# Weight conversion with a bit mask, block sums in the second pass and a plain last pair: one change to a fused attention and feed-forward kernel

## The chip, the cores and the metric

The kernel runs on one core of one Trainium2 chip. The metric is the device time of one execution in microseconds (us). The core has five engines with a queue each, and they run side by side: PE (TensorE, the matmuls; its weight loads are counted apart as PEld), DVE (VectorE), ACT (ScalarE), POOL (GpSimd) and SP (SyncE, which issues the DMAs). An instruction waits in its engine's queue until the semaphores it needs have been set.

## The reference, cut to what matters

```python
def _attn_ref(q, k, v):                      # each 4 x 12 x 448 x 64
    scores = scale * np.matmul(q, k.transpose(0, 1, 3, 2))
    scores = np.where(causal_mask, -1000000000.0, scores)
    attn = softmax(scores)                   # max taken off, sum + 1e-9
    return np.matmul(attn, v)

def _moe_ref(x, w_in, w_out):                # 1792 x 768, 768 x 2048, 2048 x 768
    h = x @ w_in
    g = h * np.cos(h)
    return g @ w_out
```

The attention's result, with heads and sequence swapped, is `x`. All tensors are drawn afresh as random numbers by the setup. The two weights come to the kernel as 64-bit words, and the kernel makes 32-bit floats of them itself.

## The kernel before, in words

**Precision.** Every operand of a feed-forward matmul is split into a high part (type fp32r) and the rest, the low part. A product is three matmuls: high by high, high by low, low by high. The high part is a cast on ACT, the low part a subtraction on POOL (`split`, L529 and L530; for weights L121 and L122).

**Attention** comes first, with an order written out by hand. It leaves `x` in SBUF: tokens 0 to 1023 in `xa`, the other 768 in `xb`. Beside it the first four weight chunks are converted and the first 512-token block of the feed-forward part is begun.

**Feed-forward part (`moe`).** The 2048 hidden columns are 16 chunks of 128, taken in 8 groups of two (`g`). For a group and a token block, `m1` makes two tiles of h (18 matmuls of 128x512 each, L513 to L515) and g = h cos h from them: ACT L518 (to an integer), DVE L519, ACT L520 and L521, DVE L522. The second layer is issued one step later (`flush` of the step before), so that the first-layer matmuls of the next block stand ahead of it. Only two h tiles and three output tiles (`o`) fit in PSUM; a tile is free when DVE or ACT has read it. From here on the tile scheduler, not the program text, sets the order of each queue.

- **Pass one** works on two token blocks of 512 (`xa`). Here `m2a` is the second layer: per 128 tokens 12 matmuls of 384 columns (L569), which DVE adds to `acc` (L555; L553 in the first group). In the same pass the other 28 weight chunks are converted, two per step (`convert_next`): load `st`, DVE L107 and L110 (exponent and sign bits moved into place), ACT L113 (a square, for the underflow test), DVE L116 (low bits) and L120 (zero if the square is too small), ACT L121 (high part), POOL L122 (low part). The parts are stored to DRAM (`w_in_d`, `w_out_d`), since pass two needs them again. For each pair of `w_out` chunks, `spill_out` also makes the four sums of blocks that pass two multiplies with: POOL L140, ACT L146, POOL L147, and eight stores.
- **Pass two** works on tokens 1024 to 1791 as blocks of 512 and 256 (`xb`). The second layer is a Strassen-Winograd product: of a 2 by 2 split in blocks, 7 products in place of 8. `factors` makes the sums of g blocks (POOL L597, splits L529 and L530), `m2b` the 7 products (L657) into `acc5` (512 tokens) or `acc2` (256). After the products of the last group, `after` combines the seven accumulators (L624 on DVE and POOL) and the results are stored.

DMAs all go through SP's queue. The weight tiles are in two sets, by the parity of the group; `wo_all` is a double buffer of the seven `w_out` blocks of a group, filled by one DMA (`reload_out`).

Of the kernel before, what the change touches and what calls it, by code (L numbers as in the profile page):

```python
# [9 lines left out]
F32 = mybir.dt.float32  # L10
# [3 lines left out]
U32 = mybir.dt.uint32  # L14
# [6 lines left out]
def kernel(  # L21
# [29 lines left out]
    W_MIN2 = 1.265625 * 2.0**-30  # L51

# [15 lines left out]
    w_out_d = spill.tile([NG, P, 7, 2, EH], F32, name="w_out_d")  # L68
# [56 lines left out]
    def spill_in(f, w):  # L125
        for u in range(2):
            nc.sync.dma_start(out=w_in_d[f, :, u, :], in_=f32(w[u][:]))

    def spill_out(g, w, raw, pool):
        b11, b12 = (raw[0][:, e * EH : (e + 1) * EH] for e in range(2))  # L130
        b21, b22 = (raw[1][:, e * EH : (e + 1) * EH] for e in range(2))
        for u in range(2):
            nc.sync.dma_start(out=w_out_d[g, :, 0, u, :], in_=f32(w[0][u][:, 0:EH]))
            nc.sync.dma_start(
                out=w_out_d[g, :, 1:3, u, :], in_=f32(w[1][u][:]).rearrange("p (e n) -> p e n", e=2)
            )

        def total(a, b):
            t = pool.tile([P, EH], F32, tag="tr", bufs=3, name="tr")
            nc.gpsimd.tensor_tensor(t, a, b, op=ALU.subtract)  # L140
            return t

        def put(n, t):
            th = pool.tile([P, EH], F32R, tag="th", bufs=2, name="th")
            tl = pool.tile([P, EH], F32R, tag="tl", bufs=2, name="tl")
            nc.scalar.copy(th, t)  # L146
            nc.gpsimd.tensor_tensor(tl, t, f32(th), op=ALU.subtract)  # L147
            nc.sync.dma_start(out=w_out_d[g, :, n, 0, :], in_=f32(th[:]))
            nc.sync.dma_start(out=w_out_d[g, :, n, 1, :], in_=f32(tl[:]))

        t3 = total(b22, b12)
        put(6, t3)
        t1 = total(b12, b11)
        put(4, t1)
        t2 = total(b22, t1)
        put(5, t2)
        put(3, total(b21, t2))
# [383 lines left out]
    def moe(ring, early):  # L541
        with (
# [14 lines left out]
            def m2a(g, t0, n, gs):  # L557
                for c in range(n // P):
# [4 lines left out]
                    for fi in range(2):  # L563
                        wh, wl = ring[1, 2 * g + fi]
                        gh, gl = gs[fi]
                        terms += [(gh, wh), (gh, wl), (gl, wh)]
                    for x, (a, w) in enumerate(terms):
                        for e in range(2):
                            nc.tensor.matmul(  # L569
                                o[:, e, 0:EH], lhsT=a[:, cs], rhs=w[:, e * EH : (e + 1) * EH],  # L570
                                start=(x == 0), stop=(x == 5),
                            )
                    add(g, acc[:, i], o[:, :, 0:EH])
                    if g == NG - 1:
                        nc.sync.dma_start(
                            out=out[i * P : (i + 1) * P, :], in_=acc[:, i].rearrange("p e n -> p (e n)")
                        )
# [37 lines left out]
            ORDER = [0, 5, 6, 4, 1, 3, 2]  # L615

            def m2b(g, t0, n, ops, wo, acc):
                h = n // 2
                nb = h // P
                last = g == NG - 1  # L620
                a = lambda k: acc[k - 1]

                def plus(d, b, eng=nc.vector):
                    eng.tensor_tensor(d, d, b, op=ALU.add)  # L624

                def store(d, r, e):
                    nc.sync.dma_start(
                        out=out[t0 + r * h : t0 + (r + 1) * h, e * EH : (e + 1) * EH].rearrange(
                            "(b p) n -> p b n", p=P
                        ),  # L630
                        in_=d,
                    )

                def after(i):
                    k = i + 1
                    if k == 1:
                        plus(a(2), a(1), nc.gpsimd)
                        plus(a(6), a(1))
                    elif k == 6:
                        plus(a(7), a(6))  # L640
                        plus(a(3), a(6), nc.gpsimd)
                    elif k == 7:
                        plus(a(4), a(7))
                    elif k == 5:
                        plus(a(3), a(5))
                        plus(a(5), a(7), nc.gpsimd)
                        store(a(5), 1, 1)
                    elif k == 2:
                        store(a(2), 0, 0)
                    elif k == 4:  # L650
                        store(a(4), 1, 0)
                    else:
                        store(a(3), 0, 1)
# [8 lines left out]
                if nb == 2:  # L662
                    for i in ORDER:
# [4 lines left out]
                        if last:  # L668
                            after(i)
# [158 lines left out]
```

## Time and profile before

| what | value |
|---|---|
| median of 3 runs | 692.94 us (691.65 to 693.1) |
| profiled execution, own time | 693.67 us |
| its span, first to last instruction | 691.9 us |
| PE busy, share of the span | 645.2 us, 93% |
| DVE busy | 503.7 us, 73% |
| POOL busy | 408.2 us, 59% |
| ACT busy | 377.8 us, 55% |
| DMA moved | 117.14 MB, 169 GB/s over the span |
| mean granted TensorE clock | 0.971 of full speed |

The shares are means over stages with different limits, so the kernel is to be read stage by stage: attention up to about 184 us, pass one to about 497 us, pass two after it. PE's share counts matmuls at half clock as busy too.

### The profile page before, as it was taken

How to read it: one execution, taken by the hardware profiler on the slowest of the kernel's cores; microseconds unless marked ns; L12 is line 12 of the kernel's file. 1: busy time of each engine (PE TensorE's matmuls, PEld its weight loads, DVE VectorE, ACT ScalarE, POOL GpSimd, SP SyncE). 2: the span in 40 equal slices, each digit the busy share in tenths (PEclk: the TensorE clock that was granted, in tenths of full speed). 3: DMA queues.
4: the chain of work that ended last, by engine and by line, in shares of the span. 5: the costliest groups of instructions: out<-in, count | busy, mean ns of one | idle time of the engine just before them, and what ended most of it. 6: DMA issues, size and time to landing. Idle time of an engine off the chain costs nothing.

```text
span 691.9 us, 11407 instructions
## 1 busy us (share of the span) xinstructions
PE 645.2 (93%) x3763; PEld 552.3 (80%) x3763; DVE 503.7 (73%) x1027; ACT 377.8 (55%) x913; POOL 408.2 (59%) x424
## 2 busy tenths in 40 slices
PE   8999999999799968899697989999999999999993
PEld 6676767676588857788596979999999999999993
DVE  5788888898386999998969786343355665565577
ACT  6898989998445445545353544322334534544450
POOL 3665666566157979788484747311436535744576
PEclk9999999999989989989998999999999999999998
DMA  5555556551366569776765652407836236524403
GB/s 132 119 122 142 141 127 166 133 139 47 105 215 216 176 228 307 230 255 196 261 210 204 202 207 91 161 1 270 312 102 249 99 154 251 203 101 200 160 1 136
DMA packets 112954, 117.14 MB, mean 169 GB/s; under 512 B 71936, under 2 KB 100096, under 8 KB 111872
## 3 DMA queue, kind: packets, MB, share of 16 engines
q1 hardware_dynamic: 111008, 115.96, 51.6%
q10 hardware_dynamic: 1888, 0.46, 0.3%
q8 instruction: 30, 0.49, 0.3%
q14 instruction: 28, 0.23, 0.1%
HBM read 76.28 MB, written 40.11 MB: 168 GB/s over the span
## 4 chain that ended last, share of the span: by engine, by line
PE 62%; DVE 18%; POOL 9%; issue 5%; DMA 4%; ACT 1%; SPq 0%; POOLq 0%; DVEq 0%
PE o L657 11%; PE h L513 7%; PE h L514 7%; PE o L569 7%; PE h L515 7%; PE bk L390 7%; PE sc L295 5%; PE sc L366 4%; DVE ct L110 4%; DVE ct L107 3%; DVE ct L116 3%; PE bk L304 3%; PE bk L268 3%; POOL tr L140 3%; DVE acc L555 2%
## 5 line engine op out<-in xcount | busy, mean ns | idle before, releaser
L555 DVE TENSOR_TENSOR acc<-acc,o 128x768 f32<-128x768 f32 (+1 forms) x136 | 122.7, 911 | 49.6 <-PE o L657 29.1
L530 POOL TENSOR_TENSOR gl<-r,gh 128x512 fp32r<-128x512 f32 (+1 forms) x56 | 64.6, 1154 | 65.5 <-ACT gh L529 59.5
L122 POOL TENSOR_TENSOR wl<-ct,wh 128x768 fp32r<-128x768 f32 (+1 forms) x40 | 68.9, 1729 | 52.3 <-ACT wh L121 52.3
L344 POOL TENSOR_TENSOR pb<-pb,stat 128x768 f32<-128x768 f32 (+2 forms) x72 | 73.9, 1040 | 41.8 <-ACT T L278 19.3
L513 PE MATMUL h<-xa,wh 128*128 128x512 f32 x192 | 77.8, 405 | 12.7 <-DVE r L522 12.7
L569 PE MATMUL o<-wh,gh 128*128 128x384 f32 x256 | 69.0, 351 | 18.1 <-DVE acc L555 17.0
L519 DVE SCALAR_TENSOR_TENSOR r<-ni,h 128x512 f32<-128x512 int32 (+1 forms) x64 | 39.6, 618 | 62.8 <-ACT ni L518 54.7
L326 ACT ACTIVATE pb<-pb,stat 128x384 f32<-128x384 f32 (+1 forms) x144 | 72.5, 512 | 15.0 <-DVE stat L312 15.0
L514 PE MATMUL h<-xa,wh 128*128 128x512 f32 x192 | 77.8, 405 | 0.0
L515 PE MATMUL h<-xa,wl 128*128 128x512 f32 x192 | 77.2, 402 | 0.0
L597 POOL TENSOR_TENSOR sm<-r 128x256 f32<-128x256 f32 (+1 forms) x32 | 19.3, 603 | 94.0 <-DVE r L522 94.0
L518 ACT ACTIVATE ni<-h 128x512 int32<-128x512 f32 (+1 forms) x64 | 34.6, 541 | 68.6 <-PE h L515 68.6
L569 PE MATMUL o<-wl,gh 128*128 128x384 f32 x256 | 68.3, 349 | 0.0
L569 PE MATMUL o<-wh,gl 128*128 128x384 f32 x256 | 67.8, 347 | 0.0
L569 PEld LDWEIGHTS o<-wh,gh 128*128 128x128 f32 x256 | 48.1, 196 | 23.3 <-DVE acc L555 20.0
L514 PE MATMUL h<-xb,wh 128*128 128x512 f32 (+1 forms) x192 | 64.7, 337 | 0.0
L515 PE MATMUL h<-xb,wl 128*128 128x512 f32 (+1 forms) x192 | 64.7, 337 | 0.0
L513 PE MATMUL h<-xb,wh 128*128 128x512 f32 (+1 forms) x192 | 64.6, 337 | 0.0
L312 DVE CUSTOM_DVE_ANT_0 pb<-sc,mask 128x384 f32<-128x384 f32 (+1 forms) x144 | 52.9, 418 | 14.8 <-PE sc L295 14.8
L657 PE MATMUL o<-wo_all,gh 128*128 128x384 f32 x224 | 56.4, 337 | 0.9 <-DVE acc L555 0.9
L520 ACT ACTIVATE r<-r 128x512 f32<-128x512 f32 (+1 forms) x64 | 37.0, 578 | 36.1 <-DVE r L519 36.1
L513 PEld LDWEIGHTS h<-xa,wh 128*128 128x128 f32 x192 | 37.7, 196 | 21.7 <-DVE r L522 10.0
(98 smaller groups left out, 1595.1 us busy)
## 6 DMA issues: line engine op xcount, KB each, us to landing
wo_all<-w_out_d SPq DMA_DIRECT2D x8, 2688.0 KB, 10.0
st<-in_moe_w_in_dram SPq DMA_DIRECT2D x14, 768.0 KB, 4.9
st<-in_moe_w_out_dram SPq DMA_DIRECT2D x14, 768.0 KB, 5.3
w_in_d<-wh SPq DMA_DIRECT2D x16, 384.0 KB, 5.2
w_in_d<-wl SPq DMA_DIRECT2D x16, 384.0 KB, 3.3
w_out_d<-th SPq DMA_DIRECT2D x32, 192.0 KB, 3.3
w_out_d<-tl SPq DMA_DIRECT2D x32, 192.0 KB, 2.8
wh<-w_in_d SPq DMA_DIRECT2D x16, 384.0 KB, 8.9
```

What stands on the lines that cost most here:

```text
L122: nc.gpsimd.tensor_tensor(wl, tf, f32(wh), op=ALU.subtract)
L312: nc.vector.tensor_tensor_reduce(out=dst, in0=src, in1=m, scale=-1.0, scalar=3.0e38, op0=ALU.add, op1=ALU.min, accum_out=st[:, 0, n : n + 1],)
L326: nc.scalar.activation(dst, dst, AF.Exp, scale=-1.0, bias=st[:, 0, n : n + 1], accum_out=st[:, 1, n : n + 1],)
L344: nc.gpsimd.tensor_tensor(dst, dst, r.to_broadcast(list(dst.shape)), op=ALU.mult)
L390: nc.tensor.matmul(o[heads(j), kc * P : S], lhsT=vn[:, kc, heads(j)], rhs=pm[:, kc, j, kc * P : S], start=(kc == 0), stop=(kc == NB),)
L513: yield nc.tensor.matmul(hv, lhsT=wh[:, f], rhs=x[:, 0, cc, t], start=(cc == 0), stop=False)
L514: yield nc.tensor.matmul(hv, lhsT=wh[:, f], rhs=x[:, 1, cc, t], start=False, stop=False)
L515: yield nc.tensor.matmul(hv, lhsT=wl[:, f], rhs=x[:, 0, cc, t], start=False, stop=(cc == NCC - 1))
L530: nc.gpsimd.tensor_tensor(lo, r, f32(hi), op=ALU.subtract)
L555: nc.vector.tensor_tensor(d, d, o, op=ALU.subtract)
L569: nc.tensor.matmul(o[:, e, 0:EH], lhsT=a[:, cs], rhs=w[:, e * EH : (e + 1) * EH], start=(x == 0), stop=(x == 5),)
L657: nc.tensor.matmul(o, lhsT=ops[i][u][:, b * P : (b + 1) * P], rhs=wo[:, i, v, :], start=(x == 0), stop=(x == 2),)
```

## The change

It has four parts.

- **Conversion (28 weights of pass one).** `convert_whole` takes the place of `convert_weight`. ACT makes a mask tile `mk` from the high word by three activations (L138, L139, L140): its 32 bits are those of a number just under 2, 0x3FFFFFFF, or zero where the weight is too small. DVE then needs three instructions: shift and mask (L142), low bits (L145), sign and top bits (L148). L107, L113 and L120 go for these weights. The high and low parts stay a cast on ACT (L152) and a subtraction on POOL (L153). `mk` has one buffer.
- **Block sums.** `spill_out` is gone from pass one. The converted chunk itself is stored (`raw_d`), reloaded in pass two (`reload_raw`), and `block_sums` makes the four sums of groups 0 to 6 there: POOL L707, ACT L708, DVE L709. A `reload_out` is three DMAs.
- **First `add` of an accumulator**: on ACT (L557) where it was on DVE (L553).
- **Last group of pass two**: eight plain products with the `m2a` of pass one, 72 matmuls of 384 columns where there were 63. `combine` (L651, all on POOL) brings the seven accumulators together before the last products are added, so that only an add and a store follow a chunk. The last chunk of the output is done and stored in two halves.

Lines move: L519, L522, L529, L530, L555, L569, L597 and L657 of before are L523, L526, L533, L534, L559, L575, L606 and L630 after.

```diff
-    def spill_out(g, w, raw, pool):
...
+    def convert_whole(st, w, pool):
+        wh, wl = w
+        lo32, hi32 = st[:, :, 0], st[:, :, 1]
+        hif = f32(hi32)
+        m = pool.tile([P, DM], F32, tag="mk", bufs=1, name="mk")
+        nc.scalar.activation(m, hif, AF.Identity, scale=SMALL, bias=edge[:, 0:1])
+        nc.scalar.activation(m, m, AF.Sign, bias=edge[:, 1:2])
+        nc.scalar.activation(m, m, AF.Copy, scale=ONES)
+        t = pool.tile([P, DM], U32, tag="ct1", bufs=3, name="ct")
+        nc.vector.scalar_tensor_tensor(
+            t, hi32, 3, m.bitcast(U32), op0=ALU.logical_shift_left, op1=ALU.bitwise_and
+        )
+        nc.vector.scalar_tensor_tensor(
+            t, lo32, 29, t, op0=ALU.logical_shift_right, op1=ALU.bitwise_or
+        )
+        nc.vector.scalar_tensor_tensor(
+            t, hi32, 0xC0000000, t, op0=ALU.bitwise_and, op1=ALU.bitwise_or
+        )
+        tf = f32(t[:])
+        nc.scalar.copy(wh, tf)
+        nc.gpsimd.tensor_tensor(wl, tf, f32(wh), op=ALU.subtract)
+        return tf
...
             def add(g, d, o):
                 if g == 0:
-                    nc.vector.tensor_scalar(d, o, -1.0, None, op0=ALU.mult)
+                    nc.scalar.activation(d, o, AF.Copy, scale=-1.0)
...
-            ORDER = [0, 5, 6, 4, 1, 3, 2]
...
+            def combine(a):
+                def plus(d, b):
+                    nc.gpsimd.tensor_tensor(a[d - 1], a[d - 1], a[b - 1], op=ALU.add)
+
+                plus(2, 1)
+                plus(6, 1)
+                plus(7, 6)
+                plus(3, 6)
+                plus(3, 5)
+                plus(5, 7)
+                plus(4, 7)
...
-                raw[key] = convert_weight([staged.pop(key)], ring[key], mo, bufs=3)
-                kind, f = key
-                if kind == 0:
-                    spill_in(f, ring[key])
-                elif f % 2:
-                    spill_out(f // 2, [ring[1, f - 1], ring[key]], [raw[1, f - 1], raw[key]], mo)
+                t = convert_whole(staged.pop(key), ring[key], mo)
+                spill_halves((w_in_d, w_out_d)[key[0]], key[1], ring[key])
+                if key[0]:
+                    spill_raw(key[1], t)
...
+            def reload_raw(g):
+                t = raws[g] = mo.tile([P, 2, DM], F32, tag="st1", bufs=2, name="wr")
+                nc.sync.dma_start(out=t, in_=raw_d[g])
+
+            def block_sums(g):
+                wo = wo_all[:, g % 2]
+                t = raws.pop(g)
+                b11, b12 = (t[:, 0, e * EH : (e + 1) * EH] for e in range(2))
+                b21, b22 = (t[:, 1, e * EH : (e + 1) * EH] for e in range(2))
+
+                def put(i, a, b):
+                    t = mo.tile([P, EH], F32, tag="tr", bufs=3, name="tr")
+                    nc.gpsimd.tensor_tensor(t, a, b, op=ALU.subtract)
+                    nc.scalar.copy(wo[:, i, 0, :], t)
+                    nc.vector.tensor_tensor(wo[:, i, 1, :], t, f32(wo[:, i, 0, :]), op=ALU.subtract)
+                    return t
+
+                put(6, b22, b12)
+                t2 = put(5, b22, put(4, b12, b11))
+                put(3, b21, t2)
...
-                    if u == 0 and g + 1 < NG:
+                    if u == 0 and not last:
                         reload_out(g + 1)
+                        if g + 1 < NG - 1:
+                            block_sums(g + 1)
+                        if g + 2 < NG - 1:
+                            reload_raw(g + 2)
...
+                    if last:
+                        if n == 512:
+                            combine([acc5[:, i] for i in range(7)])
+                            rows = [acc5[:, a : a + 2, b] for a in (1, 3) for b in range(2)]
...
+                        pend = (m2a, g, t0, n, gs, ws, rows)
```

What the scheduler makes of it is seen in the order of the instructions on an engine. A row is the line, the operation, output and inputs by their names in the program, and the shape.

The first place is DVE's queue in pass one around the last adds of `m2a` for group 1 and the first token block (`ct` is a weight under conversion, `st` its loaded words, `mk` the mask, `acc` the accumulator, `o` a PSUM output, `r` the cosine's tile). Before:

```order
L107 TENSOR_SCALAR ct<-st 128x768
L110 SCALAR_TENSOR_TENSOR ct<-st,ct 128x768
L555 TENSOR_TENSOR acc<-acc,o 128x768
L116 SCALAR_TENSOR_TENSOR ct<-st,ct 128x768
L120 SCALAR_TENSOR_TENSOR ct<-st,ct 128x768
L107 TENSOR_SCALAR ct<-st 128x768
L519 SCALAR_TENSOR_TENSOR r<-ni,h 128x512
L110 SCALAR_TENSOR_TENSOR ct<-st,ct 128x768
L116 SCALAR_TENSOR_TENSOR ct<-st,ct 128x768
L522 SCALAR_TENSOR_TENSOR r<-r,h 128x512
```

After:

```order
L142 SCALAR_TENSOR_TENSOR ct<-st,mk 128x768
L526 SCALAR_TENSOR_TENSOR r<-r,h 128x512
L145 SCALAR_TENSOR_TENSOR ct<-st,ct 128x768
L559 TENSOR_TENSOR acc<-acc,o 128x768
L148 SCALAR_TENSOR_TENSOR ct<-st,ct 128x768
L559 TENSOR_TENSOR acc<-acc,o 128x768
L142 SCALAR_TENSOR_TENSOR ct<-st,mk 128x768
L145 SCALAR_TENSOR_TENSOR ct<-st,ct 128x768
L148 SCALAR_TENSOR_TENSOR ct<-st,ct 128x768
L523 SCALAR_TENSOR_TENSOR r<-ni,h 128x512
```

A weight takes three rows of DVE where it took four, and all three read two tiles in SBUF. In the whole queue, 43 adds of `m2a` (L553, L555) stand ahead of the last conversion before; after, 36 on DVE and 8 on ACT do.

The second place is ACT's queue at the same point of pass one (`wh` with a number is the high part of one weight, `th` that of a block sum, `gh` that of g, `edge` two constants). Before:

```order
L121 CAST wh_3189<-ct 128x768
L520 ACTIVATE r<-r 128x512
L521 ACTIVATE r<-r 128x512
L113 ACTIVATE st<-st 128x768
L529 CAST gh<-r 128x512
L121 CAST wh_3201<-ct 128x768
L146 CAST th<-tr 128x384
L113 ACTIVATE st<-st 128x768
L146 CAST th<-tr 128x384
```

After:

```order
L152 CAST wh_3295<-ct 128x768
L524 ACTIVATE r<-r 128x512
L138 ACTIVATE mk<-st,edge 128x768
L525 ACTIVATE r<-r 128x512
L139 ACTIVATE mk<-mk,edge 128x768
L522 ACTIVATE ni<-h 128x512
L533 CAST gh<-r 128x512
L140 ACTIVATE mk<-mk 128x768
L524 ACTIVATE r<-r 128x512
L525 ACTIVATE r<-r 128x512
L138 ACTIVATE mk<-st,edge 128x768
L533 CAST gh<-r 128x512
```

The casts of block sums are gone and three mask activations stand where one square stood; the mask of the next weight is begun before the high part of the one before (the cast `wh_3311` comes three rows further on). The whole queue of ACT holds two ACT_TABLE_LOAD rows before, and the same two after.

The third place is POOL's queue at the end of the program (`fl` and `gl` are low parts of g factors, `sm` sums of g blocks). Before:

```order
L597 TENSOR_TENSOR sm<-r 128x128
L530 TENSOR_TENSOR fl<-r,fh 128x128 x2
L530 TENSOR_TENSOR fl<-sm,fh 128x128
L597 TENSOR_TENSOR sm<-sm,r 128x128
L624 TENSOR_TENSOR acc_5298<-acc_5298 128x768
L530 TENSOR_TENSOR fl<-sm,fh 128x128
L597 TENSOR_TENSOR sm<-r,sm 128x128
L530 TENSOR_TENSOR fl<-sm,fh 128x128 x2
L624 TENSOR_TENSOR acc_5298<-acc_5298 128x768
L624 TENSOR_TENSOR acc_5301<-acc_5301,acc_5299 128x384
L624 TENSOR_TENSOR acc_5302<-acc_5302,acc_5299 128x384
L624 TENSOR_TENSOR acc_5300<-acc_5300 128x384
```

After:

```order
L651 TENSOR_TENSOR acc_5160<-acc_5160 128x768 x3
L651 TENSOR_TENSOR acc_5161<-acc_5161 128x384
L651 TENSOR_TENSOR acc_5160<-acc_5160 128x768
L534 TENSOR_TENSOR gl<-r,gh 128x512
L651 TENSOR_TENSOR acc_5162<-acc_5162,acc_5161 128x384
L651 TENSOR_TENSOR acc_5160<-acc_5160 128x768
L651 TENSOR_TENSOR acc_5162<-acc_5162,acc_5161 128x384
L651 TENSOR_TENSOR acc_5164<-acc_5164,acc_5161 128x384
L534 TENSOR_TENSOR gl<-r,gh 128x256 x2
L651 TENSOR_TENSOR acc_5160<-acc_5160 128x768
L651 TENSOR_TENSOR acc_5162<-acc_5162,acc_5163 128x384
```

The sums and splits of the last factors are gone from the end of the queue; the combining adds (`acc_5160` is `acc5`, the others are `acc2`) stand among the splits of the last plain g tiles. Behind the rows shown come two more adds of 128x384.

## Rows read from the trace of the kernel before

**Rows 1.** Windows: us, busy us of PE, PEld, DVE, ACT, POOL; PEclk, DMA share, GB/s
```profile
200.50:410.00 209.50, 184.86 (x869) 165.46 (x868) 186.32 (x181) 100.94 (x159) 159.99 (x103) 0.93 0.68 227
410.00:496.90 86.90, 84.77 (x432) 77.18 (x431) 39.08 (x50) 32.02 (x54) 30.72 (x28) 1.00 0.47 172
496.90:660.50 163.60, 163.60 (x937) 152.85 (x936) 94.96 (x129) 71.90 (x178) 84.14 (x151) 1.00 0.43 167
660.50:691.90 31.40, 20.16 (x121) 18.61 (x119) 24.27 (x32) 7.93 (x21) 22.39 (x26) 0.91 0.21 76
```

**Rows 2.** Waits of PE, 200 to 410 us: total us, times, longest
```profile
PE o L569 <- DVE acc L555: 14.9, 6, 4.1
```

**Rows 3.** Chain of waits, 420 to 500 us: start, us, what (of five such periods)
```profile
424.36 6.26 PE o L569 x36
...
431.09 2.09 PE o L569 x12
...
490.65 6.26 PE o L569 x36
```

**Rows 4.** Timeline of PE at the first second-layer matmul of pass one
```profile
200.47 0.51 PE L569 MATMUL o<-wh,gh 128*128 128x384 f32 x2
```

**Rows 5.** Windows of 10 us in pass one, columns as in rows 1
```profile
250.00:260.00 10.00, 9.67 (x33) 8.64 (x34) 9.97 (x11) 4.53 (x7) 6.10 (x5) 0.69 0.60 194
```

**Rows 6.** DVE by line, 205 to 410 us: count, busy us, mean ns, idle before
```profile
L116 DVE SCALAR_TENSOR_TENSOR ct<-st,ct 128x768 uint32<-128x768 uint32 x25 | 34.4, 1378 | 0.2
L110 DVE SCALAR_TENSOR_TENSOR ct<-st,ct 128x768 uint32<-128x768 uint32 x24 | 33.8, 1409 | 0.3
L120 DVE SCALAR_TENSOR_TENSOR ct<-st,ct 128x768 f32<-128x768 f32 x25 | 33.5, 1342 | 0.7
L555 DVE TENSOR_TENSOR acc<-acc,o 128x768 f32<-128x768 f32 x32 | 29.9, 943 | 0.8 <-PE o L569 0.8
L107 DVE TENSOR_SCALAR ct<-st 128x768 uint32<-128x768 uint32 x24 | 27.0, 1125 | 7.6 <-POOL wl L122 7.2 <-POOL gl L530 0.3
L519 DVE SCALAR_TENSOR_TENSOR r<-ni,h 128x512 f32<-128x512 int32 x21 | 14.3, 679 | 8.8 <-ACT ni L518 8.8
```

**Rows 7.** Timeline of DVE and POOL: start, us, engine, line, operation
```profile
192.13 0.96 DVE L110 SCALAR_TENSOR_TENSOR ct<-st,ct 128x768 uint32<-128x768 uint32 x1
...
202.07 2.48 DVE L110 SCALAR_TENSOR_TENSOR ct<-st,ct 128x768 uint32<-128x768 uint32 x1
...
201.69 2.04 POOL L710 TENSOR_TENSOR wf<-wh,wl 128x768 f32<-128x768 f32 x1
```

**Rows 8.** POOL by line, 420 to 500 us, columns as in rows 6
```profile
L530 POOL TENSOR_TENSOR gl<-r,gh 128x512 fp32r<-128x512 f32 x8 | 10.3, 1292 | 36.7 <-ACT gh L529 30.7 <-issue 6.0
L147 POOL TENSOR_TENSOR tl<-tr,th 128x384 fp32r<-128x384 f32 x4 | 4.1, 1024 | 0.1
L122 POOL TENSOR_TENSOR wl<-ct,wh 128x768 fp32r<-128x768 f32 x2 | 3.6, 1842 | 1.7 <-ACT wh L121 1.7
```

**Rows 9.** ACT by line, 205 to 410 us, columns as in rows 6
```profile
L113 ACT ACTIVATE st<-st 128x768 f32<-128x768 f32 x25 | 23.0, 919 | 38.1 <-DVE ct L110 38.1
L121 ACT CAST wh<-ct 128x768 fp32r<-128x768 f32 x24 | 19.8, 832 | 26.7 <-DVE ct L120 22.4 <-PE h L514 3.3 <-PE o L569 1.0
...
L520 ACT ACTIVATE r<-r 128x512 f32<-128x512 f32 x20 | 12.6, 629 | 10.8 <-DVE r L519 10.8
```

**Rows 10.** Chain of waits, after 655 us, columns as in rows 3
```profile
663.81 0.12 PE h L513
```

**Rows 11.** POOL by line, 660 to 692 us, columns as in rows 6
```profile
L624 POOL TENSOR_TENSOR acc<-acc 128x768 f32<-128x768 f32 x3 | 6.3, 2088 | 0.0
```

**Rows 12.** Timeline around 660.5 us (PE) and the last computation (POOL)
```profile
660.50 0.51 PE L657 MATMUL o<-wo_all,fh 128*128 128x384 f32 x2
...
687.70 1.00 POOL L624 TENSOR_TENSOR acc<-acc 128x384 f32<-128x384 f32 x1 [2.48 <-DVE acc L624]
```

More of the change, by code (lines that the diff above doesn't have):

```diff
@@ L51 @@
     W_MIN2 = 1.265625 * 2.0**-30
+    SMALL = 0.47 * 2.0**15
+    MAGIC = 1.5 * 2.0**23
+    ONES = 2.0 - 2.0**-23
     wu_in = w_in.bitcast(U32)
@@ L67 @@
     w_in_d = spill.tile([NFC, P, 2, DM], F32, name="w_in_d")
-    w_out_d = spill.tile([NG, P, 7, 2, EH], F32, name="w_out_d")
+    w_out_d = spill.tile([NFC, P, 2, DM], F32, name="w_out_d")
+    raw_d = spill.tile([NG, P, 2, DM], F32, name="raw_d")
+    edge = keep.tile([P, 2], F32, name="edge")
+    nc.vector.memset(edge[:, 0:1], MAGIC)
+    nc.vector.memset(edge[:, 1:2], -MAGIC)
     def x_part(t0, n):
@@ L123, in convert_weight @@
             return tf
-    def spill_in(f, w):
-        for u in range(2):
-            nc.sync.dma_start(out=w_in_d[f, :, u, :], in_=f32(w[u][:]))
-    def spill_out(g, w, raw, pool):
[L130 to L157, printed above, removed]
@@ L562, in m2a @@
                     terms = []
-                    for fi in range(2):
-                        wh, wl = ring[1, 2 * g + fi]
-                        gh, gl = gs[fi]
+                    for (wh, wl), (gh, gl) in zip(ws, gs):
                         terms += [(gh, wh), (gh, wl), (gl, wh)]
[L567 to L571, printed above, removed]
-                            )
[L573 to L577, printed above, removed]
+                    steps = [(x, e) for x in range(6) for e in range(2)]
+                    end = (i + 1) * P == NT
+                    if end:
+                        steps = [(x, e) for e in range(2) for x in range(6)]
+                    for x, e in steps:
+                        a, w = terms[x]
+                        nc.tensor.matmul(
+                            o[:, e, 0:EH], lhsT=a[:, cs], rhs=w[:, e * EH : (e + 1) * EH],
+                            start=(x == 0), stop=(x == 5),
+                        )
+                    d = accs[c]
+                    for es in (slice(0, 1), slice(1, 2)) if end else (slice(0, 2),):
+                        add(g, d[:, es], o[:, es, 0:EH])
+                        if g == NG - 1:
+                            nc.sync.dma_start(
+                                out=out[i * P : (i + 1) * P, :].rearrange("p (e n) -> p e n", e=2)[:, es],
+                                in_=d[:, es],
+                            )
             def factors(n, gs):
@@ L613, in factors, with m2b @@
                 return ops
-            ORDER = [0, 5, 6, 4, 1, 3, 2]
[L617 to L653, printed above, removed]
+            PAIRS = [(0, 5), (1, 2), (3, 4), (6,)]
+            def m2b(g, t0, n, ops, wo, accs):
                 def product(o, i, b):
@@ L660, in product @@
                         )
-                if nb == 2:
-                    for i in ORDER:
+                if n == 512:
+                    for i in range(7):
                         o = out_pair()
@@ L666, in m2b @@
                             product(o[:, b, 0:EH], i, b)
-                        add(g, acc[i], o[:, :, 0:EH])
-                        if last:
-                            after(i)
-                else:
-                    for p in range(0, 7, 2):
-                        two = ORDER[p : p + 2]
+                        add(g, accs[:, i], o[:, :, 0:EH])
+                else:
+                    for two, d in zip(PAIRS, accs):
                         o = out_pair()
@@ L675, in m2b @@
                             product(o[:, j, 0:EH], i, 0)
-                        if last or len(two) == 1:
-                            for j, i in enumerate(two):
-                                add(g, acc[i], o[:, j : j + 1, 0:EH])
-                                if last:
-                                    after(i)
-                        else:
-                            add(g, acc_pair[p // 2], o[:, :, 0:EH])
+                        k = len(two)
+                        add(g, d[:, 0:k], o[:, 0:k, 0:EH])
+            def combine(a):
[8 more added lines that the diff above has]
+                plus(4, 7)
             staged = {}
@@ L686, in moe @@
             staged[todo[0]] = load_weight(*todo[0], mo)
-            raw = {}
             conv = list(todo)
```

64 lines of the change are left out of this document (47 added, 17 removed).

## The prediction

> **What bounds the kernel now.** I read the windows first, cut where the work changes [rows 1]. From 496.9 to 660.5 us PE is busy for 163.60 of 163.60 us at full clock: pass two is bound by PE. From 200.5 to 410 us it is busy for only 184.86 of 209.5 us at a granted clock of 0.93, while DVE stands at 186.32 and POOL at 159.99. From 410 to 496.9 PE is at 84.77 of 86.9. After 660.5 come 31.4 us in which PE works for 20.16.
>
> The waits say who holds PE in pass one: output banks that DVE has not yet added, 14.9 us in six waits [rows 2]. DVE in turn is full of conversions there: three kinds of SCALAR_TENSOR_TENSOR of 1.34 to 1.41 us, a TENSOR_SCALAR of 1.125, and adds of 0.943 [rows 6].
>
> What pass one would take at PE's pace is read where nothing waits. Four periods lie between the blocks at 424.36 and 490.65 us [rows 3], so one is 16.57 us. Its second layer is 48 matmuls of 384 columns in 6.26 + 2.09 = 8.35 us, 0.174 us each; the first layer of 512 tokens has the other 8.22 us. From the first second-layer matmul at 200.47 us [rows 4] to 490.65 + 6.26 = 496.91 PE does 16 second-layer steps but for the last quarter of one, and 15 first-layer steps (14 of pass one, one of pass two): 15.75 x 8.35 + 15 x 8.22 = 254.8 us. It took 296.4. So **41.6 us are lost to waits** in pass one. PE's idle time in the two windows is 24.6 + 2.1 = 26.7 us of them; the other 14.9 are matmuls at a lower clock after such gaps, as from 250 to 260 us, where the clock is 0.69 (a mix of 1.2 and 2.4 GHz) right after PE had waited [rows 5]. A wait that goes gives back more than its length.
>
> **Conversion and block sums: what DVE and POOL have left in pass one.** In the order, 44 adds stand ahead of the last conversion, that is 11 second-layer steps, so at PE's pace the 28 weights must fit in 11 x 16.57 = 182 us, 6.51 us each. Some are begun before 200 us, so this counts high.
>
> POOL first, since DVE's times hang on it. Gone are the sums: 28 low parts alone took 37.9 us (28 x 1.35, or 1.02 where POOL worked beside a lighter DVE [rows 8]), and the totals about as much again. Left are 28 x 1.842 + 22 x 1.292 [rows 8], and two 128x768 adds for the first spill of about 1.85: 84 us of 182, 46%, where it was 159.99 of 209.5, 76% [rows 1].
>
> The same DVE instruction took 0.96 us at 192.13 us, away from POOL's work, and 2.48 us beside a POOL addition of 128x768 [rows 7]; the three forms mean 1.376 us [rows 6]. If the excess over 0.95 follows POOL's share, it falls to 0.426 x 46 / 76 = 0.26, so 1.21 us an instruction and 3.6 us a weight. The rest of DVE is 36 adds of 0.943 (the eight first ones are ACT's now) and 44 steps of the cosine of 0.68: 64 us, 2.3 a weight. Sum 5.9 us. Before, DVE was busy for 0.89 of the window while it was the bound [rows 1]; at that share a weight takes 6.6 us against 6.51, that is 3 us over 28 weights.
>
> ACT takes on work: three activations of 0.919 (as L113) and a cast of 0.832 [rows 9] are 3.6 us a weight; 88 activations of the cosine and splits of about 0.63, and 8 first adds of about 0.83 (by the cast of that size) are 62 us, 2.2 a weight. Sum 5.8 of 6.51 us, 89%. That is covered, but ACT and DVE now hand each weight to and fro, both near nine tenths.
>
> Bounds for what is still lost in pass one: 0, if PE sets the pace throughout; and, if the new instructions keep the 1.376 us, (4.13 + 2.3) / 0.89 = 7.2 us a weight, 28 x 0.7 = 20 us. I take 6, near the low end since 28 weights in 182 us count high, but not 0 because of the two engines that wait for each other. Pass one gains 41.6 - 6 = 35.6 us.
>
> Here a rule speaks against the change. The Trainium skill, page "SBUF — State Buffer", section "Who interferes with whom", says that a DVE instruction with two SBUF inputs and a GpSimd instruction that reads SBUF exclude each other, the loser being held altogether. The 2.48 us of [rows 7] agree. By it all three new instructions are exposed, the first one more than the TENSOR_SCALAR it replaces; if the exposure, not POOL's load, decided, the loss would be the 20 us above.
>
> The mask activations take their constants from a tile. The Trainium skill, page "ScalarE: Activation LUTs", section "What ACT_TABLE_LOAD costs", gives about 93 ns for each such operand; that would be 28 x 2 x 0.093 = 5.2 us of ACT over pass one, as an estimate from the page, and no row here shows it.
>
> Memory traffic does not decide it: per group 2,688 KB of blocks become 1,536 KB of halves and 768 KB of raw words, and the DMA share is 0.68 [rows 1]; in 46 us less it would be at most 0.68 x 209.5 / 182 = 0.78.
>
> **Block sums in pass two.** Per group of 23.6 us (163.6 us hold about seven) POOL gets four instructions of 1.02 us, ACT four casts and DVE four subtractions of the same size. POOL is busy for 84.14 of 163.6 us there, DVE for 94.96, ACT for 71.9 [rows 1], so on average there is room: the cover is POOL's idle half. The reload of the raw words is issued a group ahead. What could be late is the last split of a block's factors, when the scheduler places sums ahead of it: three of them would be 3 us a group, six groups. I take 0 and keep 18 us for the range. The first adds on ACT are 7 + 4 instructions in this pass, with ACT less than half busy: 0.
>
> **The tail.** The first layer of the last 512 tokens ends at 660.50 us; 31.4 us follow [rows 12, 1]. After it the changed kernel has 36 matmuls of 0.12 us [rows 10], 21 of the products before (0.174 each), and 72 plain ones: 4.3 + 3.7 + 12.5 = 20.5 us. Then one half add, under the 0.943 us of a whole one [rows 6] (0.8 taken), and a store: from the end of the last computation (687.70 + 1.00) to the end of the span were 3.2 us. Sum 24.5, so 6.9 us less than 31.4, though nine matmuls more (1.6 us) are done. What went is the time in which the last factors, products and combining adds waited for each other. POOL's combining adds come on the path if late: six of 1.84 (2.09 by [rows 11]), seven of 128x384 at 1.02, and the splits of g are some 22 us from 660.5 on, about PE's own 20.5. I take 6, with 5 to 7.
>
> **Sum.** Against the profiled run's own time: 693.67 - 35.6 - 6 = 652.1 us. (That run is 0.7 us above the median of 692.94, which I leave inside the range.)
>
> **Rivals.**
> - *DVE stays the bound of pass one.* For it: three instructions with two SBUF inputs each, POOL still 46% busy, and masks that come late add waits to DVE's queue, where the adds that free PSUM stand behind L142 (the second place of the order shows how ACT's chain is cut by the cosine). Against: DVE's work per weight falls by over a quarter. The loss is 20 us in place of 6: 666 us, and more if the clock drops again in the gaps: 660 to 670.
> - *The moved sums hold PE in pass two.* For it: POOL's queue is in order, and every sum ahead of a split delays it by 1.02 us. Against: PE waits nowhere in pass two now and POOL is idle for 79.5 of 163.6 us, 11 us a group, against 4.1 us of new work. Price 18 us: 670.
> - *The mask chain runs one weight at a time* (the other side). `mk` has one buffer; if ACT cannot begin a mask before the weight before it is through, a weight is 3 x 0.92 + 3 x 1.38 + 0.83 = 7.7 us in series, with 2.2 us of cosine between: 9.9 us. Before, the 28 weights took 182 + 41.6 = 224 us, 8.0 each. 28 x 1.9 = 53 us more in pass one, less the 6 of the tail: about 740. It is slower from 8.2 us a weight on. Against: the order begins masks ahead of the previous cast.
> - *Nothing is gained*: the same chain at just 8 us a weight and the tail held up by POOL: 690 to 695.
>
> **Chances.** PE's pace in pass one (645 to 660): 0.66. DVE still the bound (660 to 670): 0.18. Sums in the way (660 to 675): 0.08. Serial masks: 0.05, of which 0.04 slower. Nothing: 0.03. Forecast 652 us; the likeliest case has 645 to 660 by itself, and for 8 in 10 the range is 645 to 668. A difference under 0.2% can't be told from none here; faster 0.93, same 0.03, slower 0.04.
>
> **What the changed profile would show.** Right: from 200 us on PE busy in nearly all of every 10 us at a clock of 1.0; waits for L559 (the add) under 6 us in pass one; L142, L145 and L148 near 1.2 us; POOL below half in pass one; the third quarter of the last second-layer step of pass one ended at about 461 us; pass two unchanged at 163 to 164 us; about 25 us from the last 512-token first layer to the end. Wrong: DVE above 0.9 with instructions of 1.4 us (the first rival), PE waiting for a split or a block sum in pass two (the second), or DVE idle before L142 with ACT as releaser (the third). A tail that ends with POOL rows L651 would make it a little longer.

## The result and the profile after

The changed kernel took 670.74 us (median of 4 runs, 668.8 to 672.53) against 692.3 us before (4 runs). The ratio is 0.9689, with a 95% interval of 0.9658 to 0.9721: 21.6 us or 3.1% faster. The direction was right, but 652 us were forecast with a range that ended at 668, so the gain came out at about half of the 40 us promised. The profiled execution took 672.53 us by its own time, with a span of 670.7.

The windows of the changed kernel, cut at the points that answer to [rows 1]: the first second-layer matmul, the end of the third chunk of the last second-layer step of pass one (where the first 256-column matmul starts), the end of the last 512-token first layer, the end. The columns are as there.

```profile
200.30:400.00 199.70, 183.79 (x898) 162.05 (x897) 154.89 (x155) 137.57 (x197) 88.54 (x49) 0.98 0.69 231
400.00:479.70 79.70, 79.70 (x401) 71.96 (x400) 40.76 (x52) 31.19 (x53) 31.87 (x27) 1.00 0.46 162
479.70:645.20 165.50, 164.09 (x938) 152.43 (x937) 97.47 (x138) 85.62 (x208) 109.40 (x170) 1.00 0.38 125
645.20:670.70 25.50, 20.88 (x130) 20.22 (x128) 11.96 (x18) 5.71 (x12) 19.73 (x16) 0.97 0.26 93
```

The cut points come from these lines of PE's timeline, the two below from the changed kernel:

```profile
200.31 0.51 PE L575 MATMUL o<-wh,gh 128*128 128x384 f32 x2
479.74 0.28 PE L517 MATMUL h<-xb,wh 128*128 128x256 f32 x1
...
645.21 0.51 PE L630 MATMUL o<-wo_all,fh 128*128 128x384 f32 x2
```

and this one from the kernel before:

```profile
496.76 0.28 PE L513 MATMUL h<-xb,wh 128*128 128x256 f32 x1
```

Stage by stage, for one work content of 254.8 us in pass one:

| stage | before | after | forecast for after |
|---|---|---|---|
| pass one, first to last cut | 296.3 us | 279.4 us | 260.8 us |
| of it lost to waits | 41.5 us | 24.6 us | 6 us |
| pass two | 163.7 us | 165.5 us | 163.7 us |
| tail | 31.4 us | 25.5 us | 25.4 us |

So the tail came out as forecast, pass two is 1.8 us longer, and almost the whole miss, 18.6 us, lies in pass one. DVE is no longer the bound there: 154.89 of 199.7 us, 0.78, where it was 0.89 [rows 1]. POOL has 0.44. PE nevertheless stands still for 15.9 us of the first window. What PE waited for in the changed kernel from 180 to 500 us, and then ACT, DVE and SP's queue from 190 to 400 us, each in a fence of its own (total us, times, longest):

```profile
PE h L517 <- DVE r L526: 11.5, 7, 4.0
PE o L575 <- DVE acc L559: 7.6, 6, 1.6
```

```profile
ACT mk L138 <- DMA st<-in_moe_w_out_dram: 26.9, 11, 5.5
ACT mk L138 <- DMA st<-in_moe_w_in_dram: 15.3, 9, 3.2
```

```profile
DVE ct L142 <- ACT mk L140: 14.5, 7, 4.4
DVE r L526 <- ACT r L525: 13.1, 7, 3.0
```

```profile
SPq L96 <- DVE ct L148: 57.7, 13, 10.8
```

Read from the bottom: SP's queue waits for the third DVE instruction of a weight before it issues a load; ACT's first mask activation waits 42.2 us in 20 waits for such loads; DVE waits for ACT's masks and cosines; PE waits for the cosine (L526), which has not yet freed an h tile. One turn of this loop, from the chain of waits (start, us, what):

```profile
380.88 1.65 DVE ct L148
...
382.59 5.34 DMA st<-in_moe_w_out_dram
...
388.01 1.01 ACT mk L138
...
389.74 0.50 ACT ni L522
390.24 0.77 ACT mk L139
...
391.05 0.63 ACT r L524
391.68 0.74 ACT mk L140
...
392.51 0.96 DVE ct L142
```

The load is issued within 0.1 us of L148's end and takes 5.34 us. ACT, in whose queue L138 comes next, does nothing for 5.53 us, and the cosine activation L522, whose h tile PE finished at 382.6 us, stands behind it until 389.6. DVE's timeline shows when this weight is through:

```profile
397.77 0.94 DVE L148 SCALAR_TENSOR_TENSOR ct<-st,ct 128x768 uint32<-128x768 uint32 x1
```

The buffer was held from 388.01 to 398.71, 10.7 us, after a load of 5.4. With two buffers two weights pass per turn: (10.7 + 5.4) / 2 = 8.0 us a weight in this turn. Over all 28 weights a buffer is held for 9.2 us on the mean from L138's start to L148's end (6.2 to 11.7), and from there to the first activation of the weight that takes the buffer next it is 6.1 us: (9.2 + 6.1) / 2 = 7.7. The order of SP's queue is not what delays the loads: of the 26 that had to wait for a buffer, 25 were issued within 0.5 us of the L148 that gave it back, the last after 1.4 us. Over pass one the first and the last L138 stand at 191.3 and 396.9 us, 27 weights apart: 7.6 us each, where PE's pace asked for 6.51.

### The profile page after: what moved, and what is told of

Same layout as the page of the kernel before. It is cut to its first block, busy times and chain, and to the rows that moved or that the text cites. A ratio compares the mean times of both kernels' runs of the same rounds, so it can differ in the third digit from the quotient of the medians.

```text
span 670.7 us, 11327 instructions
## 1 busy us (share of the span) xinstructions
PE 641.3 (96%) x3772; PEld 545.4 (81%) x3772; DVE 461.5 (69%) x995; ACT 427.6 (64%) x974; POOL 358.3 (53%) x378
## 4 chain that ended last, share of the span: by engine, by line
PE 64%; DVE 11%; ACT 11%; DMA 11%; issue 2%; POOL 1%; SPq 0%; DVEq 0%; ACTq 0%; POOLq 0%
PE o L630 11%; PE o L575 8%; PE h L517 7%; PE h L518 7%; PE h L519 7%; PE bk L394 7%; DMA st<-in_moe_w_in_dram 6%; PE sc L299 5%; PE sc L370 4%; DVE ct L145 3%; DMA st<-in_moe_w_out_dram 3%; PE bk L308 3%; PE bk L272 3%; ACT mk L138 2%; DVE ct L142 2%; DVE ct L148 2%
## 5 line engine op out<-in xcount | busy, mean ns | idle before, releaser
L559 DVE TENSOR_TENSOR acc<-acc,o 128x768 f32<-128x768 f32 (+1 forms) x129 | 117.8, 924 | 54.8 <-PE o L630 35.7
L534 POOL TENSOR_TENSOR gl<-r,gh 128x512 fp32r<-128x512 f32 (+1 forms) x57 | 67.1, 1179 | 122.9 <-ACT gh L533 71.0
L153 POOL TENSOR_TENSOR wl<-ct,wh 128x768 fp32r<-128x768 f32 x28 | 55.6, 1992 | 50.7 <-ACT wh L152 47.4
L519 PE MATMUL h<-xa,wl 128*128 128x512 f32 x192 | 77.5, 404 | 0.0
L575 PE MATMUL o<-wh,gh 128*128 128x384 f32 x256 | 66.0, 338 | 8.4 <-DVE acc L559 7.6
L523 DVE SCALAR_TENSOR_TENSOR r<-ni,h 128x512 f32<-128x512 int32 (+1 forms) x64 | 39.5, 617 | 48.7 <-ACT ni L522 47.3
L522 ACT ACTIVATE ni<-h 128x512 int32<-128x512 f32 (+1 forms) x64 | 34.6, 540 | 48.3 <-PE h L519 47.4
L575 PE MATMUL o<-wl,gh 128*128 128x384 f32 x256 | 65.2, 335 | 0.0
L575 PE MATMUL o<-wh,gl 128*128 128x384 f32 x256 | 65.1, 335 | 0.0
L519 PE MATMUL h<-xb,wl 128*128 128x512 f32 (+1 forms) x192 | 64.9, 338 | 0.0
L526 DVE SCALAR_TENSOR_TENSOR r<-r,h 128x512 f32<-128x512 f32 (+1 forms) x64 | 39.4, 618 | 36.7 <-ACT r L525 35.9
L138 ACT ACTIVATE mk<-st,edge 128x768 f32<-128x768 f32 x28 | 28.0, 1000 | 46.9 <-DMA st<-in_moe_w_out_dram 26.9
L575 PEld LDWEIGHTS o<-wh,gh 128*128 128x128 f32 x256 | 46.3, 188 | 13.8 <-DVE acc L559 10.5
```

Source lines behind the costliest of these rows:

```text
L153: nc.gpsimd.tensor_tensor(wl, tf, f32(wh), op=ALU.subtract)
L519: yield nc.tensor.matmul(hv, lhsT=wl[:, f], rhs=x[:, 0, cc, t], start=False, stop=(cc == NCC - 1))
L534: nc.gpsimd.tensor_tensor(lo, r, f32(hi), op=ALU.subtract)
L575: nc.tensor.matmul(o[:, e, 0:EH], lhsT=a[:, cs], rhs=w[:, e * EH : (e + 1) * EH], start=(x == 0), stop=(x == 5),)
```

## The experiments

Theory A is this loop: two buffers for the loaded words, each held through three mask activations and three DVE instructions, then a load. Theory B: DVE's instructions are still lengthened by POOL working beside them. Theory C: ACT and DVE wait for each other through the one mask tile and their in-order queues. The loss in pass one is worked out as in the table above; all times are medians, and the kernel before stood at 693.5 to 694.3 us beside them, so that ratios compare.

**e1, a third buffer for the loaded words.**

```diff
-        st = pool.tile([P, n, 2], U32, tag=f"st{parts}", bufs=2, name="st")
+        st = pool.tile([P, n, 2], U32, tag=f"st{parts}", bufs=3 if parts == 1 else 2, name="st")
...
-                t = raws[g] = mo.tile([P, 2, DM], F32, tag="st1", bufs=2, name="wr")
+                t = raws[g] = mo.tile([P, 2, DM], F32, tag="st1", bufs=3, name="wr")
```

> The changed kernel with three buffers in place of two for the loaded words (st). Theory A, the load loop: in the changed kernel a weight took 7.6 us because a load of 5.3 us is issued only when the third DVE instruction of the weight two places earlier has given its buffer back; the first mask activation waited 42 us for loads. Then these waits go (under 8 us in all), the loss to waits in pass one falls from 24.6 us to 5 to 10, and the median is 652 to 658 us. Theory B, DVE held by POOL: the third buffer changes little, 668 to 672 us, and the DVE instructions stay at 1.1 to 1.45 us. Theory C, ACT and DVE wait for each other through one mask buffer and in-order queues: L138 then waits for DVE in place of the load, and the time is 663 to 670.

657.69 us, ratio 0.9477 (0.9454 to 0.95), at the upper end of A's range. ACT's waits for loads are gone:

```profile
ACT mk L138 <- DVE ct L142: 31.1, 16, 4.4
...
ACT mk L138 <- DMA st<-in_moe_w_in_dram: 1.7, 1, 1.7
```

The loss in pass one is 465.41 - 200.32 - 254.8 = 10.3 us (A had 5 to 10), the weights take (378.2 - 191.3) / 27 = 6.9 us each, and pass two and the tail keep their 165.5 and 25.4 us. What the loads had held up is seen in the chain of waits. Its shares by line between 200 and 400 us, in the changed kernel and then in e1 (the view cuts its lines off there):

```profile
by line: DMA st<-in_moe_w_in_dram 17.0%; DVE ct L145 11.5%; DMA st<-in_moe_w_out_dram 11.3%; DVE ct L148 7.8%; ACT mk L138 7.1%; DVE ct L142 6.9%; ACT mk L139 6.2%; issue 5.2%; ACT mk L140 4.2%; DMA w_in_d<-wh 3.3%; DVE acc L559 3.2%; ACT r
```

```profile
by line: PE o L575 29.8%; PE h L518 9.8%; PE h L517 9.8%; PE h L519 9.7%; DVE ct L142 7.3%; DVE ct L145 5.4%; ACT mk L139 3.5%; ACT mk L138 3.3%; ACT mk L140 3.1%; issue 2.3%; DVE ct L148 2.1%; POOL wf L684 2.0%; DVE r L523 1.5%; DVE acc L5
```

In the changed kernel ten loads make 28% of the chain, 56.6 us, and the conversion's own instructions most of the rest; in e1 no load stands in it, and PE's matmuls make 59%. The DVE instructions did not become shorter; L142 and L145 became longer (1.13 and 1.44 us in the changed kernel, see e2):

```profile
L145 DVE SCALAR_TENSOR_TENSOR ct<-st,ct 128x768 uint32<-128x768 uint32 x25 | 40.3, 1613 | 0.4
L142 DVE SCALAR_TENSOR_TENSOR ct<-st,mk 128x768 uint32<-128x768 uint32 x25 | 35.8, 1432 | 12.4 <-ACT mk L140 5.5 <-POOL wl L153 3.4 <-issue 1.8
...
L148 DVE SCALAR_TENSOR_TENSOR ct<-st,ct 128x768 uint32<-128x768 uint32 x24 | 27.2, 1132 | 0.5
```

So theory B falls as the main cause: 13 us came back with the same contention. Of theory C the wait appeared that it named (31.1 us for L142, which still reads the one mask), but not the time.

**e2, the low parts by a memset on POOL.** This leaves the low part of the 28 weights out of the result.

```diff
-        nc.gpsimd.tensor_tensor(wl, tf, f32(wh), op=ALU.subtract)
+        nc.gpsimd.memset(f32(wl), 0.0)
```

> The changed kernel with the low part of the 28 weights set to zero by a memset on POOL in place of the subtraction (this leaves the low part out of the result). POOL then reads no weight tile beside DVE. Theory A: the three DVE instructions come near 0.95 us, the loop of a weight gets about 1 us shorter of some 15 for two weights, and L138 still waits over 25 us for loads: 655 to 664 us. Theory B: the waits of PE in pass one are gone, 648 to 655 us, and L138 waits for loads under 10 us. Theory C: 660 to 670.

667.76 us, ratio 0.9615 (0.9586 to 0.9644): 5 us less than the changed kernel by the ratios, less than A had expected and far from B; it lies in the range that C had. L138 still waited 23.1 + 16.0 us for loads, and the weights took (399.5 - 190.6) / 27 = 7.7 us each, no less than in the changed kernel. L142, L145 and L148 came to 1.06, 1.17 and 1.18 us in place of these of the changed kernel (205 to 380 us):

```profile
L145 DVE SCALAR_TENSOR_TENSOR ct<-st,ct 128x768 uint32<-128x768 uint32 x23 | 33.2, 1441 | 0.4
L148 DVE SCALAR_TENSOR_TENSOR ct<-st,ct 128x768 uint32<-128x768 uint32 x22 | 29.0, 1316 | 0.4
...
L142 DVE SCALAR_TENSOR_TENSOR ct<-st,mk 128x768 uint32<-128x768 uint32 x23 | 25.9, 1126 | 18.8 <-ACT mk L140 7.6 <-issue 5.3 <-POOL wl L153 3.0
```

Contention is there, and shortening it helps a little; it is not what sets the pace.

**e3, the new conversion alone** in the kernel before (sums in pass one, first adds on DVE, old last group); the definition of `convert_whole` and its constants come with it.

```diff
-                raw[key] = convert_weight([staged.pop(key)], ring[key], mo, bufs=3)
+                raw[key] = convert_whole(staged.pop(key), ring[key], mo)
```

> The kernel before with the new conversion alone (sums still in pass one, first adds on DVE, old last group). Theory A: the load loop paces it as in the changed kernel, but with POOL's sums beside it the DVE instructions stay near 1.4 us, so a weight takes 7.8 to 8.2 us: 685 to 695 us, nothing gained. Theory B: one DVE instruction less a weight, 28 x 1.125 = 31 us less of DVE: 670 to 680.

691.05 us, ratio 0.996 (0.9943 to 0.9977): 0.4%, as A had it, with 8.2 us a weight. L137, its first mask activation, waited 30.0 + 9.8 us for loads.

**e4, the changed kernel with the old conversion.**

```diff
-                t = convert_whole(staged.pop(key), ring[key], mo)
+                t = convert_weight([staged.pop(key)], ring[key], mo, bufs=3)
```

> The changed kernel with the old conversion (four DVE instructions, one square on ACT), all else as changed. Theory A: the buffer of the loaded words is held only for DVE's four instructions and not for three mask activations before them, so most of the gain is still there: 664 to 672 us, with waits of DVE for loads under 15 us. Theory B: DVE has 28 instructions more, 28 x 0.75 = 21 us: 680 to 690.

669.9 us, ratio 0.9654 (0.9627 to 0.9681), as fast as the changed kernel, as the intervals overlap; DVE waited 6.9 us for loads. The loss in pass one is 22.4 us. So the gain of pass one came from the parts that e4 keeps, the sums taken out of it and the first adds on ACT, and none from the mask.

**e5, the old last group.** `combine` and the plain pair go, the products and `after` of before take their place (`m2b_last`), and the sums are made for group 7 as well.

```diff
-                    if last:
-                        gs = [split(r, *g_tiles(n)) for r in gs]
-                    else:
-                        ops = factors(n, gs)
+                    ops = factors(n, gs)
...
-                        if g + 1 < NG - 1:
+                        if g + 1 < NG:
                             block_sums(g + 1)
...
-                        pend = (m2a, g, t0, n, gs, ws, rows)
+                        pend = (m2b_last, g, t0, n, ops, wo_all[:, g % 2], accs)
```

> The changed kernel with the old last group (seven products, combining adds behind them, sums of blocks for group 7 too). From the end of the last 512-token first layer to the end were 31.4 us before and 25.5 in the changed kernel. If the plain pair is worth that: 674 to 679 us. Rival: the first layer and the splits of the last group were only moved to another place, and the tail's gain is given back ahead of it: 669 to 673.

678.42 us, ratio 0.9772 (0.9752 to 0.9792). Against the changed kernel's 0.9689 that is 0.0083 x 693 = 5.8 us. The stretch from the last 512-token first layer to the end, in the windows of this kernel:

```profile
644.90:676.90 32.00, 20.04 (x121) 18.50 (x119) 25.17 (x33) 7.91 (x21) 20.51 (x25) 0.96 0.21 74
```

32.0 us where the changed kernel has 25.5, with pass two at 165.5 us in both. The tail's gain stands by itself.

**e6** is the kernel of e4 once more; the name under which it ran speaks of three buffers, but it has two, as its expectation says.

> The changed kernel with the old conversion, once more beside the others on the same chip: 668 to 672 us, as e4.

671.62 us in its one run.

**e7, two mask tiles** on top of e1.

```diff
-        m = pool.tile([P, DM], F32, tag="mk", bufs=1, name="mk")
+        m = pool.tile([P, DM], F32, tag="mk", bufs=2, name="mk")
...
-                    t = mo.tile([P, EH], F32, tag="tr", bufs=3, name="tr")
+                    t = mo.tile([P, DM], F32, tag="mk", bufs=2, name="tr")[:, 0:EH]
```

> Three load buffers and two mask buffers (the block sums' tiles share the mask's buffers in pass two, to make room). With three load buffers alone the first mask activation waited 31 us for L142, which still reads the one mask. Theory C in its small form, that this wait is on the path: 651 to 655 us. Rival, that PE's pace covers it: 656 to 659, with L138's wait for L142 under 8 us all the same.

670.59 us, ratio 0.9664 (0.9639 to 0.9688): both expected times missed, 13 us slower than e1. L138's wait for L142 did fall to 5.3 us, but the loss in pass one rose to 480.41 - 200.01 - 254.8 = 25.6 us. PE waited 12.6 us for adds, 6.07 us at once. DVE's timeline at that place:

```profile
281.97 0.94 DVE L142 SCALAR_TENSOR_TENSOR ct<-st,mk 128x768 uint32<-128x768 uint32 x1
282.95 0.96 DVE L145 SCALAR_TENSOR_TENSOR ct<-st,ct 128x768 uint32<-128x768 uint32 x1
283.83 0.95 DVE L142 SCALAR_TENSOR_TENSOR ct<-st,mk 128x768 uint32<-128x768 uint32 x1
284.69 2.56 DVE L148 SCALAR_TENSOR_TENSOR ct<-st,ct 128x768 uint32<-128x768 uint32 x1
287.18 0.94 DVE L559 TENSOR_TENSOR acc<-acc,o 128x768 f32<-128x768 f32 x1
```

and what PE was waiting for (the bracket: idle time before, and its releaser):

```profile
288.17 1.01 PE L575 MATMUL o<-wh,gh 128*128 128x384 f32 x2 [6.07 <-DVE acc L559]
```

With two masks the scheduler puts four instructions of two weights in a row ahead of the add that frees PE's bank. The add stands behind them, though PE waits for it from 282.1 us on. In e1 the one mask tile keeps the instructions of two weights apart. That the order costs this wait is seen here; that it accounts for the whole 15 us is not shown.

**e8, as e7 with the first add on DVE again.**

```diff
-                    nc.scalar.activation(d, o, AF.Copy, scale=-1.0)
+                    nc.vector.tensor_scalar(d, o, -1.0, None, op0=ALU.mult)
```

> As e7, with the first add of an accumulator on DVE again. In pass two of the changed kernel PE waited 1.4 us once, for a cosine behind block sums and first adds on ACT. If the first adds caused it: pass two 1 to 2 us shorter, 1 to 2 us less than e7. Rival: DVE's eight adds more in the first group of pass one cost as much: within 1 us of e7.

673.27 us, ratio 0.9699 (0.9684 to 0.9713): 2.7 us more than e7 by the medians, with intervals that just overlap. Neither expectation held; having the first adds off DVE is worth a little at most. The loss in pass one is 27.0 us. Pass two takes 163.9 us in e7 and 164.1 in e8, with PE busy throughout, whether the first adds are on ACT or on DVE.

**e9, the old conversion with the third buffer.**

```diff
-        st = pool.tile([P, n, 2], U32, tag=f"st{parts}", bufs=2, name="st")
+        st = pool.tile([P, n, 2], U32, tag=f"st{parts}", bufs=3 if parts == 1 else 2, name="st")
...
-                t = convert_whole(staged.pop(key), ring[key], mo)
+                t = convert_weight([staged.pop(key)], ring[key], mo, bufs=3)
...
-                t = raws[g] = mo.tile([P, 2, DM], F32, tag="st1", bufs=2, name="wr")
+                t = raws[g] = mo.tile([P, 2, DM], F32, tag="st1", bufs=3, name="wr")
```

> The old conversion with three buffers for the loaded words, all else as changed. With two buffers the old conversion was as fast as the new one (669.9 against 670.7 us). If the third buffer helps only the new conversion, because only there loads are late (42 us of waits against 7): 666 to 671 us, and the mask is worth 9 to 13 us once loads are early. Rival: the third buffer helps by itself, whatever the conversion: 655 to 661 us.

675.39 us, ratio 0.9737 (0.9712 to 0.9761), outside both expected ranges: 17.7 us slower than e1, and by the intervals slower than e4, its own form with two buffers. The loss in pass one is 28.9 us. The four ratios side by side:

| | two load buffers | three load buffers |
|---|---|---|
| old conversion | 0.9654 (e4) | 0.9737 (e9) |
| new conversion | 0.9689 (the changed kernel) | 0.9477 (e1) |

So the third buffer does nothing good by itself; and the mask, worth nothing with two buffers, is worth more than expected with three, 0.026 of the time. Against e4, which has neither, the two together give 0.018.

**e10, e1 with the first adds of pass two on DVE** and those of pass one left on ACT.

```diff
-            def add(g, d, o):
-                if g == 0:
+            def add(g, d, o, first=nc.scalar):
+                if g == 0 and first is nc.vector:
+                    nc.vector.tensor_scalar(d, o, -1.0, None, op0=ALU.mult)
+                elif g == 0:
...
-                        add(g, accs[:, i], o[:, :, 0:EH])
+                        add(g, accs[:, i], o[:, :, 0:EH], nc.vector)
...
-                        add(g, d[:, 0:k], o[:, 0:k, 0:EH])
+                        add(g, d[:, 0:k], o[:, 0:k, 0:EH], nc.vector)
```

> Three load buffers, with the first adds of pass two on DVE and those of pass one left on ACT. The wait of 1.4 us in pass two follows a cast of a block sum that waits for POOL on ACT, with the cosine behind it. If the first adds on ACT had a part in it, 655.5 to 657 us; if it is the cast alone, the same as with three buffers alone, 657 to 658.5.

662.6 us, ratio 0.9548 (0.9529 to 0.9566), 5 us slower than e1: missed on both sides. Pass one loses as little as in e1 (9.2 us), but pass two is 4.6 us longer (170.1 us), with a new wait:

```profile
PE o L632 <- ACT gh L533: 4.9, 5, 1.0
```

The best kernel of the study is e1, 5.2% faster than before.

## Why the prediction was wrong, point by point

**The bound of pass one** was read rightly: DVE held PE and 41.6 us were lost. DVE went from 0.89 to 0.78 of the window.

**The step that failed is "Memory traffic does not decide it", and with it the bounds of 0 to 20 us for what is still lost.** The share of the DMA engines was forecast at most 0.78 and is 0.69; as a bandwidth it decides nothing. But the sum took each engine's busy time for a weight (5.9 us on DVE, 5.8 on ACT) and compared it with 6.51 us. It had no line for the time that one weight holds its load buffer. In the kernel before, DVE's L107 opened the hold, with one square on ACT inside it, and it lasted for 7.3 us on the mean to the end of L120. In the changed kernel three activations on ACT, cut by the cosine, come first, the hold lasts for 9.2 us, and the load of 5.3 us comes in series with all of it. That loop gives 7.6 us a weight and a loss of 24.6 us, outside the bounds; with a third buffer the same kernel loses 10.3 us, and 657.69 us lies within the forecast's range. What part of these 14.3 us is the loop's own is not shown, since an edit moves the scheduler's order too (e7, e9, e10); the loads' 28% of the chain, gone in e1, speak for the loop.

**The rivals.** The first (DVE stays the bound) has about the right time, 666, with the wrong mechanism: DVE is at 0.78, and e1 speeds the kernel up while L145 grows to 1.61 us, so the near hit of its price is luck. The third (serial masks through one `mk`) had the right place, ACT's first activation ahead of the cosine, and the wrong resource: the load buffer and not the mask. A second mask tile, on top of the third load buffer, made it slower (e7).

**The size of the DVE instruction.** Forecast were 1.21 us at 46% POOL; measured are 1.30 us on the mean (88.1 us in 68) at 44%, and in e1 1.40 us (103.3 us in 74) at 49%, more than the 1.376 us of before at 76%. So the excess did not follow POOL's share, as the forecast let it, and this cost less than the forecast's bound: e1 loses 10.3 us, not 20. The Trainium skill, page "SBUF — State Buffer", section "Who interferes with whom", says that a DVE instruction with two SBUF inputs contends with a GpSimd instruction that reads SBUF. The runs agree that the effect exists (L142 of 2.58 us at 384.26 in the changed kernel, beside POOL's L153 from 381.82 to 386.03, and of 0.94 at 281.97 in e7, with POOL idle; a mean of 1.14 in e2, where the largest of POOL's reads are gone).

**ACT's price.** The three activations were taken at 0.919 us each. They took:

```profile
L138 ACT ACTIVATE mk<-st,edge 128x768 f32<-128x768 f32 x23 | 23.0, 999 | 34.0 <-DMA st<-in_moe_w_out_dram 19.2 <-DMA st<-in_moe_w_in_dram 13.4 <-DVE r L526 0.7
L139 ACT ACTIVATE mk<-mk,edge 128x768 f32<-128x768 f32 x23 | 21.5, 935 | 0.2
L140 ACT ACTIVATE mk<-mk 128x768 f32<-128x768 f32 x23 | 19.3, 840 | 0.2
```

Their sum, 2.77 us, is that of the forecast. Between L139, with a constant from `edge`, and L140, without, lie 95 ns. The Trainium skill, page "ScalarE: Activation LUTs", section "What ACT_TABLE_LOAD costs", gives about 93 ns for such an operand; the trace agrees, though the two activations differ in their function as well (Sign and Copy).

**Pass two** was taken at 0 and cost 1.8 us, of which 1.4 are one wait of PE for a cosine. The chain of waits of the changed kernel shows its place:

```profile
509.53 1.02 POOL tr L707
510.57 0.51 ACT wo_all L708
511.08 0.32 ACT r L524
```

A cast of a block sum waits on ACT for POOL, and the cosine stands behind it. It is the second rival's mechanism at a tenth of its price. In e7 and e8, where the sums' tiles share the two mask buffers, PE has no such wait, and of the 1.8 us 0.1 to 0.3 are left.

**The tail** was forecast at 6 us and measured at 5.9 in the trace and 5.8 in e5. Its terms hold too: PE is busy for 20.88 us where 20.5 were summed, and from the end of the last add (667.61 us) to the end of the span it is 3.1 us where 3.2 were taken.

**What stays open.** e7 to e10 show that small edits move the scheduler's order and with it 3 to 18 us. Why the old conversion loses more with three buffers than with two was not followed to its cause, and neither was what sets the last 10 us of e1. The pace of the weights alone does not give the loss: in e7 they took (383.45 - 190.98) / 27 = 7.1 us each, less than in the changed kernel, and the loss is 25.6 us.

## What to carry to other kernels

When work is moved from one engine to another, add up not only each engine's busy time but the time that one item holds its buffers, from the load's issue to the last reader, and divide by the number of buffers: here (9.2 + 6.1) / 2 = 7.7 us a weight stood against 6.51 at PE's pace, in a stage in which DVE, ACT and POOL were all under 0.8 busy. A DMA share well under 1 says nothing about a load that is issued too late. An instruction that may wait for a load should not stand in a queue ahead of work that something faster is waiting for, and edits that are worth nothing alone (the mask, the third buffer) may be worth 1.8% together, so such parts are to be tried together.

## What the runs showed of the hardware that was not expected

Nothing of the chip itself was new here: loads of 768 KB took 5.3 us with the DMA engines at 0.69, and activations, adds and matmuls had the durations of before. New was that DVE instructions with two SBUF inputs grew (L142 from 1.13 to 1.43 us, L145 from 1.44 to 1.61; L148 fell from 1.32 to 1.13) when conversion ran faster in e1, with POOL at 97.64 of 199.7 us in place of 88.54, and that the kernel became 13 us faster all the same.
